# Transposes back on TensorE, key scales also on GpSimd, a six-piece fold and a new instruction order in an RWKV + Fourier-mix kernel

## The chip, the cores and the metric

One Trainium2 chip, one of its cores. The metric is device time in microseconds (us) of one execution, the median over runs. Engines: PE (TensorE: matmuls and transposes; its weight loads are a row of their own, PEld), DVE (VectorE), ACT (ScalarE), POOL (GpSimd), SP (SyncE, which here only issues transfers). DMA engines carry all transfers; SP, ACT and POOL each have a queue that issues them in order.

## The reference

Shapes: batch 4, 8 heads, sequence 768, head size 48, model width 384 (8 x 48), hidden width 1536.

```python
# stage 1: linear attention with a decaying state, per batch and head
cur = np.einsum('bhd,bhe->bhde', u[None] * kt, vt)
y[:, :, t] = np.einsum('bhd,bhde->bhe', rt, state + cur)
state = w[None, :, :, None] * state + np.einsum('bhd,bhe->bhde', kt, vt)
# stage 2: x is y with its heads side by side, 4 x 768 x 384
X = np.fft.fft(np.fft.fft(x, axis=1), axis=2)
u = x + np.real(X).astype(np.float32)
un = (u - mean(u)) / np.sqrt(var(u) + 1e-06)
out = u + np.maximum(un @ w_ch1, 0.0) @ w_ch2
```

## The kernel before

**Stage 1** works on 24 chunks of 128 positions, six to a batch (i = 6b + q). A chunk's keys (and, for batches 1 to 3, its queries) are loaded as f32 into `kr`, its values into `vt`. KR scales keys and queries by powers of the decay (768 elements a partition; K1 is the form for keys alone, 384). V casts the values. The scaled rows have to be turned, so that the head's elements lie on partitions: KRT is the turned tile. For batch 0 PE turns four pairs of heads (tp4; the queries go another way, tp6 and QT6). For later chunks there are two ways: PE with eight transposes into a PSUM bank (tp8) and a copy out of it on ACT or DVE, or one transposing transfer on SP's queue straight from KR to KRT (xbar8), with no PE work and no copy. Then PE makes the scores (A), and each of their two halves is masked, either by ACT's copy AC and POOL's select MA, or by DVE alone (MA); PR multiplies turned keys and queries for the bonus term (PE `de`, ACT DE, TT on POOL or DVE); u and S carry the state; qs, y and X finish the chunk.

**Stage 2**, a batch at a time: the six chunks of X are folded three times (EO: first half of the sequence plus or minus second half; HH: first half of the width plus or minus second; XF: the same with mirrored columns), all on DVE or POOL. For batch 0 the fold runs in thirds, each from two chunks (q and q + 3). Then come PE's first transform fp (four groups g, three parts each), its copy TT2, mirrored copies TR, and the second transform mp with the residual (xr, UF). UB centres the rows, st and MV make the variance. The centred rows have to be turned too (UNT): for the two halves of batch 0 by PE, three transposes for each block of 128 rows (tq) and a copy; for the other six halves by one transposing transfer on SP's queue (xbar9).

**The MLP** takes a half batch (384 rows, hf = 0 to 7) at a time: twelve hp groups of three matmuls 128x384, each followed by HT (ReLU) on ACT or DVE; then for each of three row blocks four mo groups of three matmuls, osb on DVE, and a transfer out. W1 and W2 are loaded and cast by transfers on POOL's queue, three pieces each.

**Order.** Nothing schedules at run time. Each call of `op` appends a numbered operation with its alternatives (engine, form). The list ORDER names every operation once: `1109@4` is operation 1109 on PSUM bank 4, `493.1` operation 493 in its second alternative, a `NONE` alternative emits nothing. One list gives all engines their order; each engine runs its own instructions in that order and waits for what it needs. `idle` operations are matmuls of zeros; as many are emitted as the list names. A tile name such as kr or KR is a ring of buffers (kr has six), handed out in the list's order.

The lines that matter below: L424 KR, L462 tp8, L468 xbar8, L478 PR, L493 A, L502/L505 MA, L661 fp, L736 tq, L753 xbar9, L773 hp, L793 mo, L819 W1, L804/L805 transfers out.

Of the kernel before, what the change touches and what calls it, by code (L numbers as in the profile page):

```python
# [15 lines left out]
H = 8  # L16
S = 768
D = 48
# [9 lines left out]
XBAR_HALVES = frozenset(range(2, 8))  # L28
# [69 lines left out]
211 182.1 188 150 173 151 157 227 171 159 180 155 176.1 229 208 160 187.1 169 167 178 168 231 174.1 158 152@0 161 181  # L98
153 185 156 205 172.1 184 170 162 179 177.1 154 165 163 233 186.1 164 235 215.1 189 196 197 200 212 201 175 216 198
218 166 199 214 190 228 213 192 295 0@1 1@1 2@1 3@1 4@1 5@1 6@1 7@1 8@1 9.1@1 219@1 194 221@2 230 217 297@3 220 313  # L100
225@4 332 315@5 222 232 223@6 351 334@7 226 298.1 353@0 316.1 236 378 224 335 299.2 317.1 10@1 11@1 12@1 13@1 14.2@1
300@1,2 303.1 234 318@5,4 319.1 193 207 210 304.1 307@6 321 301.1 380@3 237 325@1 296 322 320.1 302.1 326 308 314 15@5
16.1@5 17.2@5 305@5 239 306.1 354.1 327 355.2 18@4 19@4 20@4 356@4,2 359.1 202 333 240 309 323 360.1 363@0 328 203 357
206 310.1 248 381 324 311 352.2 364 337@4,2 340.1 336.2 312.1 358 382.2 195 238 21@7 22.2@7 383@7,6 365 341.1 344@3
379 342 345 384 386.1 338.1 390@4 249 405 329.1 330 191 346 407@6 391 242 408 209 392 343 243 183 387.1 361@5 366
362.1 339.1 385 367.1 241 347 368 409.2 331.1 388 393 430 369.1 348.1 293 349 394.1 350.1 245 370 395 389.1 371
410@7,2 413.1 411.1 250 432@6 372.1 414.1 406 415@1 412.1 396.1 244 416 204 23@0 24@0 25@0 418 417.1 373 26@0 27.1@0
419.1 486 420 433 374 28@0 29@0 30.2@0 488@0 376 397 431 246 398 421.1 448 31@2 32.2@2 440@3 489 294 400 33@2 34.1@2
450@5 399 251 377 491@7,4 404 451 375 247 422 811@2 403 823@6 423 492 424 453@1,0 254 402 441.1 425 815@5 401 428 816
449 427 812 429 819@4 426 456 820 434 821 255 813 467 824 825 814 817 822 457 826.1 252 35.1@1 36.2@1 435@1,2 438.1  # L110
487 493 439.1 469@4 818 253 442@6 1062 468 827 829@1 452 494 436.1 830.1 828 257 458 443 454 460@5 437.1 841@7 444 470
842.1 459 463 269 1061 445.1 524 861@0 831.1 867@2 1063 258 477 843.1 490 855@4 856 505 862.1 461 868.1 446 498@1 478
462 507.1@7 857 863.1 832 844 835@0 836 495 526.1@3 508.1 499 447.1 455 501 858 496@4 837 464.1 500 869.1 527.1
510@6,7 511.1 465 513 849@0 509 875@2 502.1 838 512.1 528.1 503 517@3 466.1 851@6 850 853@7 504.1 876 529@5,0 497 870
472@2,1 473.1 854 532 520 852 879@7 474.1 518 506.2 880.1 256 471.1 864 37.2@5 515 534@6 1067@5 1089@1 270 514 530.1
531.1 475 833 1068.1 1069@7 1090 859 519 521 479@0 266 1083@2 1070 834 480 877@5 533 535 516.1 522 1081@1 260 481.1
1084 1077@7 476 878.1 482 483 261 537 525 1065 541 484 1109@4 536 538 267 1079@2 1110 1131@5 1078 542.1 1125@4 1064
539 557 559.2 1129@7 485 560.2 871 1071@0 523 1072 540 263 1075@3 1132 544 1073@0 1130 545 546 1121@6 547 543 1127@5
1122 550 1117@7 632 1082 1123@6 1080 1118 548 1085@1 551 264 1074 549 1087@2 1124 552 1111@7 1128 553 272 575 1126
634@0 1086 1115@6 1076 554 1119@5 262 1088 561.1 577.1@4 259 1066 555 556 273 1112.1 881@1 882 1120.1 883 893@3 894  # L120
265 613 615.2 895 885@2 578.1 635 884 889@0 896 890 891 886 887 616.2 1097@7 888 839 562@5,1 892 580@3,4 897 563 1098
898 860 1116 1113@2 594 596.2 583 899@0 900 920@1 921 1114 579 597.2 569@6 901 581 1091@3 922 570 926@2 927 582 911@0
912 840 268 905@4 906 564 913 932@1 933 1092 558.2 928 565 584 1103@0 845 576 907 587@2 923 566 567@5 1104 846 568 847
571 572 1139@4 902 1105 588 908 651 653.2 585 590 1099 586.1 848 589 591 934 573 1100 914 872 574 617.1 1106 595 919
935 592 1107 604 1093 636.1 593 618@1,6 271 605 1094 621 274 1101 1140 929 622 654.2 1095 625@0 637@2,5 626 619 638.1
598.1 599@1,7 628 614 1145@3 1096.1 600 644@6 627 629 1141 280 940 620 640.1 639.1 602.1 641.1 603.1 623@5 1151@7
624.1 606@2 601 1161@1 1152.1 607 633 275 630 608 915 1146 645 652 631 1163@7 646 1162.1 647 648 281 642 1164 865
1167@0 668.1 643 656@1,7 649 276 669 659 657.1 609 610 655 1173@5 1168 650 660 611 1147 278 866 671 661@1 1171@0 612
662 1174 663 1102.1 664 665 658.1 1153@6 282 1155@2 1108 674 670 284 1201@5 675 1156 666 873 1193@7 1154 667 1165@2
1194 672 285 1207@6 676 1202 673 1195@1 1166 677 679 1208 1159@7 678 287 680 1169@5 681 1133@2 1170 683 279 1142 1160  # L130
682 1172 1134 903 1196 684 686.2 941@6 942 943 949@5 1148 944 721 723.2 687.2 945@7 703 946 1211@0 740 742.2 953@1
1135 288 1212.1 950 951 724.2 1136 952 702 704.2 947 954 955 948 1203@6 874 743.2 1143 956 1209@0 1149 1213@5 688 277
689@7,4 957 958.1 1204 1199@1 290 904 916 759 761.2 1210 1157@3 692 291 1197@6 1200 725.1 1137 1214 980@0 981 959@7
960 1198 286 982 992@1 993 693 1158 696@2 961 1181@5 690 283 994 965@6 966 697 962 691 909 726@0,3 745@7,4 746.1 748.1
685.2 1138.1 729 910 986@1 987 747.1 1144.1 1182 698 699 705.2 924 971@0 972 727 744.1 694@4 967 1183 695.1 988 1175@3
1150 983.1 989 733@6 712 700 749.1 734 1187@1 741.2 995 973 722.2 1176 713.1 1000 730 701 752@7 1188 968 735 1177 974
1189 917 778 780.2 753 979 731 1178 1184 732 754 936 762.2 707@0,2 736 737 706 710 755 756 1190 918 925 937 708 1185
1287@4 781.2 1179 709 1277@0 1191 714@2 728 1215@5 715 289 757 716 1299@3 1216 1186.1 758 717 718 292 1235@1 795.1
1180.1 738 750@5 1236.1 1278 1288 1300 1192.1 796.1 1291@7 739 764@0,4 765.1 711 783@3,1 784.1 766.1 767 786.1 1205@6
763.1 751.1 719 1253@0 720 760 1245@4 801.1 1254.1 1206 1251@2 975 1285@6 785.1 768 1252 769 771@0 1257@2 782 772 1246  # L140
770 773 1247@1 779 963 788@4 1258 774 775 791 964 1229@5 802 789 1292 787.1 790 792 1279@2 976 776 1297@7 1280 777
1248 793 984 1239@3 1298 797.1 794 1217@2 1286.1 1281@0 798.1 1237@1 800 1289@7 799 803 1249@4 805.1 1290 1230 1238
1283@6 1240 806 804 1295@7 807 1218 809 1296 808 1231 810 1243@1 1250.1 1001@3 1002 1284.1 1005@7 1006 1007 1244.1
1013@4 1003 1014 985 969 1015 1009@6 1232 1004.1 1016 1010 1008.1 1011 1223@1 1012 930 1219 1282 931 1017 1241@4 1018
1019@3 1020 1255@7 1021 1025@6 1026 1022.1 1031@0 1032 1027 1220 1033 1224 1028 1046@3 1047 1034.1 938 1242 1225 970
# [22 lines left out]
def kernel(  # L168
# [242 lines left out]
    def attend(i):  # L411
# [449 lines left out]
```

## Time and profile before

| | |
|---|---|
| median of three runs | 174.62 us (173.65 to 176.54) |
| the profiled execution | 176.04 us, its span 174.3 us |
| granted PE clock, mean | 0.997 |
| busy: PE, DVE, ACT, POOL | 160.1, 139.9, 104.5, 71.1 us |
| MLP matmuls (L773, L793) | 2 x 288, 327 and 326 ns mean |
| transposes for KRT on PE (L462) | 64, 220 ns mean |
| transposes for UNT on PE (L736) | 18, 220 ns mean |
| first transform (L661) | 96, 248 ns mean |
| KR, K1 on DVE (L424, L419) | 18 at 1,051 ns, 6 at 547 ns |
| masks on DVE, on POOL (L505, L502) | 23 at 677 ns, 25 at 670 ns |
| PR on DVE, on POOL (L478) | 9 at 409 ns, 9 at 1,166 ns |
| TT on POOL, on DVE (L566) | 22 at 913 ns, 2 at 559 ns |
| V cast on POOL (L434) | 6 at 507 ns |
| KRT copies on ACT, on DVE (1,024 elements) | 5 at 1,050 ns, 3 at 676 ns |
| transposing transfers to KRT, to UNT | 10 at 4.6 us, 6 at 4.5 us to landing |
| loads of K, V, R | 24, 24, 18 of 192 KB; 4.3, 4.1, 4.6 us to landing |

A matmul's mean holds its latency in the pipeline, so the mean is longer than the distance between two of a row; that distance is read from the chain of waits, where a row of matmuls stands as one piece. A PE that is "busy" is therefore not necessarily at work all the time. Instructions of the other engines overlap their neighbours by some 0.06 us.

### The profile page before, as it was taken

How to read it: one execution, taken by the hardware profiler on the slowest of the kernel's cores; microseconds unless marked ns; L12 is line 12 of the kernel's file. 1: busy time of each engine (PE TensorE's matmuls, PEld its weight loads, DVE VectorE, ACT ScalarE, POOL GpSimd, SP SyncE). 2: the span in 40 equal slices, each digit the busy share in tenths (PEclk: the TensorE clock that was granted, in tenths of full speed). 3: DMA queues.
4: the chain of work that ended last, by engine and by line, in shares of the span. 5: the costliest groups of instructions: out<-in, count | busy, mean ns of one | idle time of the engine just before them, and what ended most of it. 6: DMA issues, size and time to landing. Idle time of an engine off the chain costs nothing.

```text
span 174.3 us, 4274 instructions
## 1 busy us (share of the span) xinstructions
PE 160.1 (92%) x1595; PEld 110.8 (64%) x1595; DVE 139.9 (80%) x351; ACT 104.5 (60%) x248; POOL 71.1 (41%) x106
## 2 busy tenths in 40 slices
PE   4888798789999999999999998899999999999991
PEld 1384574578676787677666765567687666666550
DVE  6498999999988998889899899569989975441632
ACT  4968999799984986685657884566433050423000
POOL 8605760178962125997300596876200001100110
PEclk9999999999999999999999999999999999999998
DMA  5999798999999999999999899870001604210323
GB/s 139 289 202 207 152 220 208 239 188 212 207 168 204 172 133 220 130 209 217 230 223 154 187 246 244 120 201 4 0 0 30 177 8 104 95 45 0 125 101 137
DMA packets 91558, 26.79 MB, mean 154 GB/s; under 512 B 86977, under 2 KB 90178, under 8 KB 91538
## 3 DMA queue, kind: packets, MB, share of 16 engines
q1 hardware_dynamic: 89568, 22.19, 65.4%
q0 software_dynamic: 1440, 3.74, 10.1%
q10 hardware_dynamic: 530, 0.59, 0.9%
q8 instruction: 12, 0.20, 0.5%
q14 instruction: 8, 0.07, 0.1%
HBM read 19.77 MB, written 4.72 MB: 140 GB/s over the span
## 4 chain that ended last, share of the span: by engine, by line
PE 58%; DMA 14%; DVE 12%; issue 5%; POOL 5%; ACT 3%; SPq 1%; DVEq 0%; ACTq 0%; POOLq 0%
PE bank L773 22%; PE bank L793 21%; DMA W<-in_moe_w_ch_dram 5%; DMA HT<-in_r_dram 3%; PE bank L661 3%; DMA KRT<-KR 3%; DMA kr<-in_r_dram 3%; PE bank L700 2%; POOL TT L566 2%; PE bank L493 2%; PE bank L578 2%; DVE HH L609 2%; DVE MA L505 2%; PE bank L384 1%; DVE KR L424 1%
## 5 line engine op out<-in xcount | busy, mean ns | idle before, releaser
L773 PE MATMUL bank<-early,W 128*128 128x384 bf16 x288 | 55.0, 327 | 0.3 <-DMA W<-in_moe_w_ch_dram 0.2
L793 PE MATMUL bank<-W,HT 128*128 128x384 bf16 x288 | 54.4, 326 | 0.0
L778 ACT ACTIVATE HT<-bank 128x384 bf16<-128x384 f32 x71 | 31.1, 501 | 24.7 <-PE bank L773 24.7
L773 PEld LDWEIGHTS <-W 128*128 128x128 bf16 x288 | 30.8, 114 | 13.2 <-DMA W<-in_moe_w_ch_dram 0.5
L793 PEld LDWEIGHTS <-HT 128*128 128x128 bf16 x288 | 26.8, 98 | 14.7
L566 POOL TENSOR_TENSOR TT<-V,DE 128x384 bf16<-128x384 bf16 x22 | 19.9, 913 | 7.7 <-ACT DE L565 4.0
L502 POOL TENSOR_SCALAR_AFFINE_SELECT MA<-AC 128x512 bf16<-128x512 bf16 x25 | 16.4, 670 | 14.8 <-ACT AC L500 10.6
L800 DVE SCALAR_TENSOR_TENSOR osb<-bank,rstd,UF 128x384 f32<-128x384 f32 x24 | 13.9, 610 | 9.7 <-PE bank L793 9.6
L804 POOL DMA_DIRECT2D out_dram<-osb x7 | 3.9, 556 | 43.2 <-DVE osb L800 43.2
L424 DVE TENSOR_TENSOR KR<-kr,wtab 128x768 bf16<-128x768 f32 x18 | 18.8, 1051 | 0.9 <-DMA kr<-in_r_dram 0.9
L779 DVE TENSOR_SCALAR HT<-bank 128x384 bf16<-128x384 f32 x25 | 13.2, 550 | 7.6 <-PE bank L773 6.9
L478 POOL TENSOR_TENSOR PR<-KRT 128x512 bf16<-128x512 bf16 x9 | 10.4, 1166 | 20.3 <-DMA KRT<-KR 20.2
L500 ACT CAST AC<-bank 128x512 bf16<-128x512 f32 x25 | 14.6, 594 | 6.5 <-PE bank L493 4.2
L505 DVE TENSOR_TENSOR MA<-bank,mtri 128x512 bf16<-128x512 f32 x23 | 15.0, 677 | 0.7 <-PE bank L493 0.6
L719 ACT ACTIVATE UB<-UF,sm 128x384 bf16<-128x384 f32 x20 | 12.0, 614 | 3.3 <-DVE UF L712 3.2
L726 DVE BATCH_NORM_STATS2 st<-UF 128x6 f32<-128x384 f32 x24 | 12.9, 546 | 0.0
L586 DVE TENSOR_TENSOR X<-bank,TT 128x384 bf16<-128x384 f32 x15 | 8.3, 550 | 4.7 <-PE bank L578 4.7
L661 PE MATMUL bank<-te_t,XF 128*128 128x193 bf16 x96 | 10.4, 248 | 0.8 <-DVE XF L624 0.8
L284 PE MATMUL bank<-zero 128*128 128x512 bf16 (+2 forms) x38 | 10.5, 398 | 0.6 <-DVE PR L481 0.5
L712 DVE SCALAR_TENSOR_TENSOR UF<-bank,X 128x384 f32<-128x384 f32 x20 | 10.5, 545 | 0.7 <-PE bank L700 0.7
L669 ACT CAST TT<-bank 97x386 bf16<-97x386 f32 x13 | 7.3, 600 | 6.2 <-PE bank L661 6.1
L661 PEld LDWEIGHTS <-XF 128*128 128x128 bf16 x96 | 8.0, 98 | 2.8 <-DVE XF L624 1.4
(113 smaller groups left out, 256.1 us busy)
## 6 DMA issues: line engine op xcount, KB each, us to landing
kr<-in_k_dram SPq DMA_DIRECT2D x24, 192.0 KB, 4.3
vt<-in_v_dram SPq DMA_DIRECT2D x24, 192.0 KB, 4.1
kr<-in_r_dram SPq DMA_DIRECT2D x18, 192.0 KB, 4.6
out_dram<-osb SPq DMA_DIRECT2D x17, 192.0 KB, 2.1
W<-in_moe_w_ch_dram POOLq DMA_DIRECT2D x6, 384.0 KB, 6.1
out_dram<-osb POOLq DMA_DIRECT2D x7, 192.0 KB, 2.3
te_t<-te_c SPq DMA_DIRECT2D x1, 579.0 KB, 5.1
HT<-in_r_dram SPq DMA_DIRECT2D x1, 576.0 KB, 4.1
```

The lines of the kernel that those rows point to most:

```text
L424: one(("KR", i), "DVE", "KR", lambda: nc.vector.tensor_tensor(out=KR().rearrange("t s p (a d) -> t (s p) a d", a=2)[:, :, :, 0:D], in0=kr( ...
L500: op(("AC", i, a), [("ACT", "AC", lambda: nc.scalar.copy(AC(), A_ps[a]())), ("NONE", "", None)], r=[("A", i)], w=[("AC", i, a)], new=[AC], ...
L502: op(("MA", i, a), [("POOL", "MA", lambda: nc.gpsimd.affine_select(out=MA[a](), in_=AC(), pattern=[[0, NP], [1, 128]], base=0, channel_mul ...
L505: ("DVE", "MA", lambda: nc.vector.tensor_tensor(out=MA[a](), in0=A_ps[a](), in1=mtri.unsqueeze(1).to_broadcast([128, NP, 128]), op=AluOp.m ...
L566: op(("TT", i), [(e, key, lambda g=g: g.tensor_tensor(out=TT(), in0=V(), in1=DE().unsqueeze(2).to_broadcast([128, H, D]), op=AluOp.mult)) ...
L661: nc.tensor.matmul(fp()[:, par, :], lhsT=XF()[:, par, nb, g * CH:g * CH + 128], rhs=te_t[:, g % 2, nb, par, :], start=(nb == 0 and par == ...
L726: one(("st", b, blk), "DVE", "st", lambda: nc.vector.bn_stats(out=st(), in_=UF()[:, j, :]), r=[("UF", b, blk)], new=[st], use=[UF])
L773: nc.tensor.matmul(hp(), lhsT=W1[:, dt, ft // 4 * 512:(ft // 4 + 1) * 512].rearrange("k (m j) -> k m j", j=4)[:, :, ft % 4], rhs=UNT()[:, ...
L778: op(("HT", hf, ft), [("ACT", "HT", lambda: nc.scalar.activation(out=HT()[:, ft, :], in_=hp(), func=Act.Relu, scale=-1.0)), ("DVE", "HT", ...
L779: ("DVE", "HT", lambda: nc.vector.tensor_scalar(out=HT()[:, ft, :], in0=hp(), scalar1=-1.0, scalar2=0.0, op0=AluOp.mult, op1=AluOp.max))],
L793: nc.tensor.matmul(mo(), lhsT=HT()[:, ft, j * 128:(j + 1) * 128], rhs=W2[:, ft, :], start=(ft == 0), stop=(ft == 11))
L800: one(("osb", hf, j), "DVE", "osb", lambda: nc.vector.scalar_tensor_tensor(out=osb(), in0=mo(), scalar=rstd()[:, j:j + 1], in1=UF()[:, j, ...
```

## The change

Five things change in the code, and the order list is new.

1. The transposing transfers go: KRT has only its two copies from PSUM, tp8 is always issued, and all eight halves of the MLP rows are turned by tq.
2. KR can run on POOL as well, whole (KRg, K1g), or be split into keys and queries on two engines (KR and KR2).
3. UB can run on POOL (UBg).
4. Batch 0's fold has no sequence step EO. Each chunk q is folded over the width alone as soon as it is there (HHn, then XFn, two instructions each, six times). The plus and minus over the sequence halves is left to PE: the first transform now sums six parts in place of three, the last three with the table `te_t` or its negated odd part `tn_t`, which one instruction (`tn`) makes. EO and HH of the other batches can run on DVE only.
5. The ring kr has five buffers for six.

```diff
-XBAR_HALVES = frozenset(range(2, 8))
...
+    tn_t = const([128, 2, 3, 193], BF16, "tn_t")
...
-    ring("kr", 6, [128, 2, H, D], F32)
+    ring("kr", 5, [128, 2, H, D], F32)
...
+        def scaled(g, s):
+            return g.tensor_tensor(
+                out=KR()[:, s].rearrange("t p (a d) -> t (p a) d", a=2)[:, :, 0:D], in0=kr()[:, s],
+                in1=wtab[ph][:, s].rearrange("t (h d) -> t h d", d=D), op=AluOp.mult)
...
+            op(("KR", i), [(e, key, lambda g=g: scaled(g, 0)) for e, key, g in (("DVE", "K1", nc.vector), ("POOL", "K1g", nc.gpsimd))],
...
+            op(("KR", i), [("DVE", "KR", lambda: both(nc.vector)), ("DVE", "K1", lambda: scaled(nc.vector, 0)),
+                           ("POOL", "K1g", lambda: scaled(nc.gpsimd, 0)), ("POOL", "KRg", lambda: both(nc.gpsimd))],
+               r=need, w=[("KR", i)], new=[KR], use=[kr])
+            op(("KR2", i), [("NONE", "", None), ("POOL", "K1g", lambda: scaled(nc.gpsimd, 1)),
+                            ("DVE", "K1", lambda: scaled(nc.vector, 1)), ("NONE", "", None)],
...
-            op(("tp", i), [("PE", "tp8", transposes), ("PE", "tp8", transposes), ("NONE", "", None)], r=[("KR", i), "ident"],
-               w=[("tp", i)], new=[tp], uses=[[KR], [KR], []])
+            one(("tp", i), "PE", "tp8", transposes, r=[("KR", i), ("KR2", i), "ident"], new=[tp], use=[KR])
...
-                            ("SP", "xbar8", lambda: nc.sync.dma_start_transpose(
-                                out=KRT().rearrange("d s p t -> d (s p) t"), in_=KR().rearrange("t s p c -> t (s p c)")))],
...
+    def narrow(q):
+        X, HHt, XF = bat[0]["X"], bat[0]["HH"], bat[0]["XF"]
+        e, n = divmod(q, 3)
+        def hid(h, alu):
+            op(("HH", 0, q, h), [(en, "HHn", lambda g=g: g.tensor_tensor(
+                out=HHt()[:, h, e, n, 0:192], in0=X()[:, q, 0:192], in1=X()[:, q, 192:384], op=alu))
...
+        def sym(h, alu):
+            grp = (slice(0, 4, 3), slice(1, 3, 1))[h]
+            op(("XF", 0, q, h), [(en, "XFn", lambda g=g: g.tensor_tensor(
+                out=XF()[:, e, n, 0:4 * CH].rearrange("t (g c) -> t g c", g=4)[:, grp], in0=HHt()[:, :, e, n, 0:CH],
+                in1=HHt()[:, :, e, n, 192:192 - CH:-1], op=alu)) for en, g in (("DVE", nc.vector), ("POOL", nc.gpsimd))],
...
+                        e, n = divmod(nb, 3)
+                        lhsT, rhs = XF()[:, e, n], (tn_t[:, g % 2, n, :] if e and par else te_t[:, g % 2, n, par, :])
...
+                ("POOL", "UBg", lambda: nc.gpsimd.tensor_scalar(
+                    out=UB()[:, j, :], in0=UF()[:, j, :], scalar1=-float(DM), scalar2=sm()[:, j:j + 1], op0=AluOp.mult,
...
-            if 2 * b + sh in XBAR_HALVES:
-                one(("UNT", b, sh), "SP", "xbar9", lambda UB=UB, UNT=UNT: nc.sync.dma_start_transpose(
...
+            for j in range(3):
+                turned(sh, j, UB, UNT)
...
+    op("tn", [("ACT", "tn", lambda: nc.scalar.mul(tn_t, te_t[:, :, :, 1, :], -1.0)),
```

The two order lists, with each number traced to its operation and alternative, hold (operations before -> after):

| operation | all | ahead of the first hp |
|---|---|---|
| PE tp8 (8 transposes), tq (3) | 8 -> 18, 6 -> 24 | 6 -> 6, 5 -> 6 |
| PE fp (2 matmuls), xr | 48 -> 60, 4 -> 5 | 12 -> 24, 4 -> 5 |
| PE y, qs, de | 24, 20, 24, as before | 9 -> 11, 8 -> 10, 11 -> 12 |
| PE idle | 38 -> 25 | 38 -> 25 |
| DVE KR, K1 | 18 -> 9, 6 -> 1 | 6 -> 3, 6 -> 1 |
| POOL KRg, K1g | 0 -> 9, 0 -> 5 | 0 -> 3, 0 -> 5 |
| MA on DVE, on POOL | 23 -> 29, 25 -> 19 | 13 -> 20, 7 -> 3 |
| PR and PRp on DVE, PR on POOL | 14 -> 21, 10 -> 3 | 9 -> 12, 3 -> 0 |
| DVE EO, HH, HHn, XFn | 18 -> 18, 21 -> 18, 0 -> 10, 12 -> 11 | 6 -> 0, 5 -> 0, 0 -> 10, 12 -> 11 |
| POOL EO, HH, HHn, XFn | 6 -> 0, 3 -> 0, 0 -> 2, 0 -> 1 | 0, 1 -> 0, 0 -> 2, 0 -> 1 |
| DVE KRT, S, TR, QT6 | 3 -> 10, 10 -> 9, 7 -> 2, 0 -> 2 | 2 -> 4, 5 -> 2, 2 -> 0, 0 -> 2 |
| DVE UNT copies, TTd, UB, UF, X, st | 4 -> 9, 2 -> 3, 4 -> 5, 20 -> 19, 15, 24 | 4 -> 2, 1 -> 2, 0 -> 1, 2 -> 1, 0 -> 1, 0 -> 1 |
| POOL UBg, TT | 0 -> 9, 22 -> 21 | 0 -> 1, 8 -> 9 |
| transfers out on SP, on POOL | 17 -> 13, 7 -> 11 | none |

Ahead of the first hp, SP's queue has K0 to K4 behind one half of batch 0's queries before; after, it has K0 and V0 ahead of that half. The third piece of W1 stands in POOL's queue directly behind KRg of chunk 11. The first MLP operations are hp (0,7), (0,10), then (0,0).

## The prediction

> **What bounds the kernel now.** I read the slices first, then the stretches, then the chain of waits from the first MLP matmul on, then the groups and single instructions of the stage ahead of it.
>
> ```profile
> PE   4888798789999999999999998899999999999991
> PEclk9999999999999999999999999999999999999998
> DMA  5999798999999999999999899870001604210323
> ```
>
> TensorE (PE) is full from the eleventh slice (44 us) to the last, at its full clock; the DMA engines are full for the first 29 slices.
>
> ```profile
> 20.00:30.00 10.00, 9.15 (x140) 6.10 (x139) 9.70 (x22) 9.29 (x22) 3.54 (x5) 1.00 0.89 197
> 30.00:40.00 10.00, 8.38 (x111) 6.52 (x111) 9.83 (x29) 8.98 (x21) 4.58 (x6) 1.00 1.04 208
> 40.00:47.00 7.00, 6.57 (x121) 5.09 (x118) 7.00 (x18) 6.72 (x19) 6.78 (x9) 1.00 1.12 215
> 47.00:60.00 13.00, 12.74 (x115) 9.21 (x115) 11.46 (x28) 9.67 (x27) 4.69 (x7) 1.00 1.08 178
> 60.00:80.00 20.00, 19.57 (x240) 14.70 (x239) 17.75 (x44) 15.44 (x37) 14.36 (x19) 1.00 1.10 181
> 80.00:100.00 20.00, 19.78 (x198) 13.99 (x197) 18.32 (x46) 13.71 (x33) 5.20 (x8) 1.00 1.03 200
> 100.00:120.00 20.00, 18.46 (x212) 12.63 (x210) 16.36 (x38) 12.53 (x34) 15.39 (x20) 1.00 0.92 180
> ```
>
> After the stretch and its length the columns are busy us of PE, weight loads, DVE, ACT, POOL, then clock, DMA share and GB/s. From 20 to 47 us DVE is busy 26.53 of 27 us: it sets the pace there. From 47 us on PE is, idle only 0.26 + 0.43 + 0.22 + 1.54 = 2.45 us up to 120 us and not at all from there to 169.95 us.
>
> ```profile
> 39.10 8.08 DMA W<-in_moe_w_ch_dram
> 47.23 1.33 PE bank L773 x7
> ...
> 60.28 0.45 PE bank L462 x8
> 60.72 2.05 PE bank L661 x24
> ...
> 108.74 4.94 DMA KRT<-KR
> ...
> 158.73 11.23 PE bank L793 x69
> ```
>
> Start, length, what: the chain crosses from the W1 load to PE at 47.23 us and stays mostly on PE. Here stand PE's issue prices, free of the latency in the groups' means: 11.23/69 = 0.163 us for an MLP matmul (0.49 a group of three), 0.45 for eight transposes (0.056 each), 2.05/24 = 0.085 for a fold matmul (0.17 a group of two).
>
> The first MLP matmul (order group hp) starts at 46.57 us, the last ends at 169.95: 123.4 us. By such prices the PE order holds from there on 192 MLP groups (94.1 us), 36 fold groups (6.2), 18 mp x 0.33 (5.9), 12 A x 0.28 (3.4), 15 y x 0.20 (3.0), 12 qs x 0.18 (2.2), ten state updates (2.1), 13 bonus groups x 0.10 (1.3), two tp8 (0.9) and one tq (0.17): **119.2 us of work, 4.2 of gaps**. What counts is when the first MLP matmul starts, what PE still has to do then, the gaps, and the tail (174.30 - 169.95 = 4.35 us).
>
> **The change part by part.**
>
> *Transposes back on PE.* Ten tp8 x 0.45 = 4.5 us and eighteen tq x 0.17 = 3.0 us. All ten tp8 and seventeen tq (2.8) stand behind the first MLP matmul. There nothing hides them, PE being full. The new order also puts two y, two qs and one bonus group, 0.86 us, ahead of that point. Remaining PE work: 119.2 + 4.5 + 2.8 - 0.9 = **125.6 us, +6.4**.
>
> The row for these transposes is 0.45 us for eight at a granted clock of 1.00. [...]
>
> *First fold in six narrow pieces.* Twelve fold groups more, 2.05 us of PE, and one more xr (0.16), all ahead of the first MLP matmul. PE's order has 22.9 us of work there now, in 46.6 us, and 26.2 after; thirteen idle matmul groups (38 to 25) make room. DVE's pace hides it; without that cover it is 3.2 us.
>
> *DVE ahead of the first MLP matmul.* By the groups' means: less KR 3 x 1.051 and K1 5 x 0.547 (-5.9, to POOL), EO 6 x 0.377 and HH 5 x 0.389 (-4.2), S, TR, UF, UNTj (-3.6); more HHn 10 x about 0.257 (as XFn, 196 elements; +2.6), MA 7 x 0.677 (+4.7), KRT 2 x 0.676 (+1.4), PR and PRp 3 x 0.41 (+1.2), two QT6 (about 0.5 each, from KRT's 0.676 for 1,024 elements), and TTd, UB, X, st (+2.2). Small rest -0.1. Net **about -0.7 us**: the scales leave, masks take their place. ACT gets about 2 us lighter, with one tn of about 1.1 (1,158 elements against KRT's 1.05 for 1,024).
>
> *W1.* These loads sit in POOL's queue, which now holds five K1g, three KRg and fewer MA and PR ahead of the third piece. K1g and KRg have no row. Bounds: the V cast, 507 ns for 384 elements with one input, gives 1.0 for KRg's 768; PR's 1,166 ns for 512 with two inputs gives 1.75. I take 1.75, and 0.9 for K1g (TT, 913 for 384). The last KRg is directly ahead of the third W1 piece; behind it wait that load, the TT of chunks 7 to 10 and then the first MLP matmul. In the shared order that piece has moved behind some 1.6 us more DVE work. Today it is issued at 39.1 and lands at 47.2, when PE is just ready. I take +1.2 us for the first MLP matmul; bounds -1 (DVE 0.7 lighter, and POOL done with its scales in time) and +3 (one KRg late on its load too).
>
> [...]
>
> *Gaps.* The ten KRT and six UNT transfers (4.6 and 4.5 us to landing) leave the DMA queue. What PE can win is bounded by the gaps: 1.5 of its idle time names KRT transfers. Against that DVE gets tighter: from the first MLP matmul to the last batch's fold it has about 74 us of work against PE's 77 (67.5 against 74.5 before). And POOL slows DVE:
>
> ```profile
> 34.14 2.13 POOL L502 TENSOR_SCALAR_AFFINE_SELECT MA<-AC 128x512 bf16<-128x512 bf16 x2 [7.86 <-ACT AC L500]
> ...
> 34.40 1.38 DVE L424 TENSOR_TENSOR KR<-kr,wtab 128x768 bf16<-128x768 f32 x1
> ```
>
> Two masks took 2.13 where a pair takes 1.22 elsewhere, and the KR beside them 1.38 where others take 0.95: 0.43 us for a collision. Fourteen scales on POOL could cost DVE 0 to 6 us; most would fall in its 3 us of slack. I take -1.5 for the transfers and +1.5 for this: gaps unchanged, bounds -3 and +4.
>
> *At nothing:* UBg on POOL (nine, about 0.5, replacing ACT's 0.614), TR moved to ACT (0.83 against 0.35, eight in all), the shorter kr ring (five for six; the load order hides it while K and R arrive at 200 GB/s; a late load costs one kr transfer, 4.6 us), outputs between SP and POOL. UNT copies need banks and 18 x about 0.4 us of ACT or DVE, inside ACT's free time.
>
> Sum on the span: 174.3 + 6.4 + 1.2 + 0 = 181.9. The profiled execution took 176.04, 1.74 around its span, and would become 183.6; the median lies 1.42 under it. **Prediction: 174.62 + 7.6 = 182.2 us.**
>
> **The rivals.**
>
> *1. The gaps close* (12%). With no transfer to wait for, the gaps fall from 4.2 to about 1 and the first MLP matmul is on time: 174.62 + 6.4 - 3.2 = 177.8, within 2%. For it: POOL's 20.2 us of waiting for KRT. Against: PE itself waited only 1.5 us of that.
>
> *2. The first MLP matmul comes early: not slower* (8%). DVE idles 0.91 + 1.54 + 1.25 + 0.58 = 4.3 us up to 13.8 us, waiting for queries and their tables, and POOL scaling keys beside it could fill this. If all of it went and the gaps closed too, 174.62 + 6.4 - 4.3 - 3.2 = 173.5. It decides from 6.4 us up, for which both must succeed; to be 2% faster needs 9.9 us, more than both bounds. Against: K0 and V0 now stand ahead of SP's query load, which the DVE idle of 1.25 waits for.
>
> *3. POOL becomes late* (8%). Its in-order queue holds KRg in front of TT and MA; if six KRg behind the first MLP matmul each delay a score chain by 1 us that PE cannot fill, 182.2 + 6 = 188.
>
> That the transposes would not move to PE is ruled out by the decoded order.
>
> **How the numbers follow.** Forecast 72%, rivals 12, 8 and 8. The 2% that a measurement can tell is 3.5 us: 171.1 to 178.1. Faster takes most of rival 2 for what rows of one execution cannot bound (6%); same is rival 1 and the rest of 2 (14%); slower is the forecast and rival 3 (80%). The forecast alone spans 178 to 187 (bounds of start and gaps, not all at once). The range takes in rival 1 and part of 2 below and most of rival 3 above: 175.5 to 188, leaving out some 15%.
>
> **What would show it.** The tp8 line should count 144 transposes and the tq line 72, at 0.056 us of issue each; PE's work from the first MLP matmul on 125 to 126 us; that matmul at 46 to 49 us; KRg at 1.6 to 2.1 us; POOL's waits for KRT gone. The forecast falls if the first MLP matmul starts before 43 us or if PE's end minus that start is under 122 us.

## The result and the profile after

The kernel after takes **182.22 us** (median of 4 runs, 181.99 to 183.76), the kernel before, beside it, 174.55 (4 runs): ratio **1.048, 95% interval 1.040 to 1.056**, slower. The profiled execution took 182.13 us with a span of 180.3 us; the spans differ by 6.0 us, the medians by 7.7, because the profiled execution of before lies 1.5 us above its median. Executions of one kernel lie 2 to 9 us apart, in part with a lower mean granted clock and in part without one (the kernel before took 174.47 and 177.98 us at 1.00), so ratios and intervals compare the faster executions (two to four of each new kernel; where only one was left, no ratio is given), and the clock stands beside a time where it matters.

The slices of the kernel after (4.5 us each):

```profile
PE   3976888849999999999999999999999999999991
PEclk9999999997999999999999999999999999999998
DMA  5999899999989589978712210110010201200333
```

PE is full from the tenth slice on (40.6 us), but the ninth holds a 4, an idle time, and in the tenth the clock has a dent. The DMA engines are nearly idle from the twenty-first slice on (before: from the twenty-eighth; the prediction read them as full for 29 slices, they are for 27), because the turns have left them and the loads are earlier.

The stretches, with the columns of the prediction:

```profile
30.00:40.00 10.00, 7.41 (x106) 6.01 (x104) 9.93 (x18) 7.65 (x18) 7.19 (x7) 1.00 1.06 203
40.00:47.00 7.00, 6.30 (x81) 5.31 (x80) 5.92 (x13) 4.54 (x16) 2.80 (x5) 0.76 1.12 216
47.00:60.00 13.00, 12.62 (x147) 9.54 (x143) 12.51 (x30) 10.57 (x28) 4.36 (x5) 1.00 0.93 182
60.00:80.00 20.00, 20.00 (x265) 15.65 (x264) 18.85 (x49) 18.41 (x42) 16.24 (x20) 1.00 0.97 187
80.00:100.00 20.00, 20.00 (x209) 14.13 (x208) 18.15 (x50) 12.55 (x28) 9.94 (x12) 1.00 0.47 112
100.00:120.00 20.00, 20.00 (x252) 15.27 (x250) 18.90 (x47) 11.37 (x32) 13.64 (x21) 1.00 0.13 49
```

From 60 to 120 us PE is busy 60.00 of 60 us (57.81 before). Before 47 us it is worse off: 7.41 of 10 us against 8.38, and then 7 us at a clock of 0.76.

The chain of waits:

```profile
37.08 2.96 DVE PR L490
...
49.68 1.14 PE bank L792 x6
...
60.72 0.45 PE bank L477 x8
...
162.42 14.15 PE bank L812 x87
```

The first MLP matmul starts at 49.68 us (46.57 before), the last ends at 176.56, and 3.69 us follow. In the kernel before the last one ends at 170.43, and 3.90 us follow:

```profile
167.82 2.60 PE L793 MATMUL bank<-W,HT 128*128 128x384 bf16 x15
```

The prediction's 169.95 is where the chain of waits leaves PE, 0.5 us ahead of its last matmul; so the stretch before was 123.9 us with 4.7 of gaps, not 123.4 with 4.2, and the tail 3.90, not 4.35. A turn of keys, L477, is 0.45 us for eight on the chain, as it was; an MLP matmul 14.15/87 = 0.163. By the prediction's prices the new order holds 125.6 us of work behind the first MLP matmul; the stretch is 126.9, so the gaps, which are the stretch less the priced work, are 1.3 us. In spans: first MLP matmul +3.1, work +6.4, gaps -3.4, tail -0.2, together +5.9.

The groups that the change touches:

```profile
L477 PE MATMUL bank<-ident,KR 128*128 128x128 bf16 x144 | 11.4, 224 | 0.5 <-DVE KR L432 0.5
L760 PE MATMUL bank<-ident,UB 128*128 128x128 bf16 x72 | 7.4, 219 | 0.0
L432 POOL TENSOR_TENSOR KR<-kr,wtab 128x768 bf16<-128x768 f32 x9 | 17.2, 1907 | 0.0
L432 DVE TENSOR_TENSOR KR<-kr,wtab 128x768 bf16<-128x768 f32 x9 | 8.5, 966 | 0.0
```

144 and 72 transposes, as decoded. POOL's whole scale takes 1.91 us, twice DVE's 0.97.

Why the first MLP matmul is late shows in single instructions of DVE and POOL:

```profile
36.41 0.67 DVE L517 TENSOR_TENSOR MA<-bank,mtri 128x512 bf16<-128x512 f32 x1
37.00 3.04 DVE L490 TENSOR_TENSOR PR<-KRT 128x512 bf16<-128x512 bf16 x1
39.96 1.28 DVE L517 TENSOR_TENSOR MA<-bank,mtri 128x512 bf16<-128x512 f32 x2
...
36.74 1.18 POOL L841 DMA_DIRECT2D W<-in_moe_w_ch_dram  x2
37.94 1.81 POOL L432 TENSOR_TENSOR KR<-kr,wtab 128x768 bf16<-128x768 f32 x1
39.69 0.57 POOL L841 DMA_DIRECT2D W<-in_moe_w_ch_dram  x1
...
40.70 0.49 PE L721 MATMUL bank<-hid_t,TR 97*128 97x192 bf16 x4 [2.53 <-DVE MA L517]
```

A PR that takes 0.41 us elsewhere takes 3.04 and ends 0.3 us behind POOL's scale of chunk 11. The masks behind it free the banks that PE's next group needs: PE idles 2.53 us up to 40.70. W1's third piece was issued at 39.69 and nothing waited for it.

### The profile page after: what moved, and what is told of

It reads as the page before. It is cut to its first block, busy times and chain, and to the rows that moved or that the text cites. A ratio compares the mean times of both kernels' runs of the same rounds, so it can differ in the third digit from the quotient of the medians.

```text
span 180.3 us, 4560 instructions
## 1 busy us (share of the span) xinstructions
PE 165.5 (92%) x1741; PEld 118.5 (66%) x1741; DVE 147.2 (82%) x372; ACT 106.3 (59%) x251; POOL 79.2 (44%) x110
## 4 chain that ended last, share of the span: by engine, by line
PE 75%; DVE 16%; DMA 3%; issue 2%; ACT 1%; SPq 1%; DVEq 0%
PE bank L792 26%; PE bank L812 26%; DVE MA L517 5%; PE bank L721 4%; PE bank L477 4%; PE bank L682 4%; DMA HT<-in_r_dram 3%; PE bank L505 2%; DVE PR L490 2%; PE bank L760 2%; PE bank L591 2%; DVE KR L432 1%; PE bank L574 1%; DVE W L378 1%; DVE XF L621 1%
## 5 line engine op out<-in xcount | busy, mean ns | idle before, releaser
L823 POOL DMA_DIRECT2D out_dram<-osb x11 | 6.3, 574 | 47.5 <-DVE osb L819 42.8
L514 POOL TENSOR_SCALAR_AFFINE_SELECT MA<-AC 128x512 bf16<-128x512 bf16 x19 | 12.3, 655 | 21.0 <-ACT AC L512 17.8
L517 DVE TENSOR_TENSOR MA<-bank,mtri 128x512 bf16<-128x512 f32 x29 | 18.9, 679 | 0.5 <-PE bank L505 0.4
L432 POOL TENSOR_TENSOR KR<-kr,wtab 128x768 bf16<-128x768 f32 x9 | 17.2, 1907 | 0.0
L682 PE MATMUL bank<-te_t,XF 128*128 128x193 bf16 x108 | 12.6, 248 | 0.8 <-ACT X L601 0.4
L512 ACT CAST AC<-bank 128x512 bf16<-128x512 f32 x19 | 10.8, 598 | 4.1 <-PE bank L505 2.1
L477 PE MATMUL bank<-ident,KR 128*128 128x128 bf16 x144 | 11.4, 224 | 0.5 <-DVE KR L432 0.5
L477 PEld LDWEIGHTS <-KR 128*128 128x128 bf16 x144 | 9.3, 100 | 1.4 <-DVE KR L432 0.6
L448 ACT CAST V<-vt 128x384 bf16<-128x384 f32 x19 | 9.7, 516 | 0.7 <-PE bank L591 0.7
L287 PE MATMUL bank<-zero 128*128 128x512 bf16 (+2 forms) x25 | 7.6, 411 | 2.5 <-DVE PR L493 1.4
```

What stands on the lines that cost most here:

```text
L432: return g.tensor_tensor(out=KR().rearrange("t s p (a d) -> t (s p) a d", a=2)[:, :, :, 0:D], in0=kr().rearrange("t s (p a) d -> t (s p) a ...
L477: nc.tensor.transpose(tp()[:, s, p, :], KR()[:, s, p, :], ident)
L514: op(("MA", i, a), [("POOL", "MA", lambda: nc.gpsimd.affine_select(out=MA[a](), in_=AC(), pattern=[[0, NP], [1, 128]], base=0, channel_mul ...
L517: ("DVE", "MA", lambda: nc.vector.tensor_tensor(out=MA[a](), in0=A_ps[a](), in1=mtri.unsqueeze(1).to_broadcast([128, NP, 128]), op=AluOp.m ...
L682: nc.tensor.matmul(fp()[:, par, :], lhsT=lhsT[:, g * CH:g * CH + 128], rhs=rhs, start=(nb == 0 and par == 0), stop=(nb == last and par == ...
```

## The experiments

Each kernel was timed beside the kernel before, whose median was 176.1, 176.4, 176.8 and 175.9 us in the four sets; ratios compare best. "Stretch" is from the first MLP matmul to the end of the last, "idle" PE's idle time in it, both of the profiled execution: 123.9 and 2.4 before, 126.9 and 0.3 after. (Idle counts only time in which no matmul stands in the profile; the gaps above count all time that the prices do not explain.)

**PE work alone** (`before_more_pe`): the kernel before with 6.4 us of matmuls of zeros added behind the first MLP matmul, a 160-column one in each of 96 mo groups.

```diff
+                if ft == lo:
+                    nc.tensor.matmul(mo()[:, 0:160], lhsT=zero[:, 0:128], rhs=W2[:, ft, 0:160], start=False, stop=False)
```

> The kernel before, with one matmul of zeros of 160 columns added to each of the 96 second MLP groups (the sums stay the same). By the prices 160 columns cost 0.067 us, so PE gets 6.4 us more work behind the first MLP matmul and nothing else changes. Theory 'work' (PE is full there, the change's 6.4 us of work is its loss): +6.4 us on the kernel before, about 181. Rival 'gaps' (the 4.2 us of gaps take the work up, the loss came with the late start and with POOL): +2.2 us at most, under 177.

183.03 us, ratio 1.037 (1.026 to 1.047), which on 174.55 is +6.4 us (4.6 to 8.3). Stretch 130.1, 6.3 longer, idle 2.7. PE's work is on the path one for one, and the gaps do not close because PE has more to do: what waits in the order of before waits as long.

**The turns doubled** (`turns_twice`): the kernel after with the ten added tp8 and eighteen added tq issued twice.

```diff
-                for s in range(2):
+                for _ in range(2 if i in (12, 14, 15, 17, 18, 19, 20, 21, 22, 23) else 1):
...
-                for dt in range(3):
+                for _ in range(2 if b else 1):
```

> The changed kernel, with the turns that the change brought to PE (ten groups of eight, eighteen groups of three) made twice into the same bank. Theory 'work': 10 x 0.45 + 18 x 0.17 = 7.5 us more, about 189.7. [...]

191.94 us, ratio 1.089 (1.073 to 1.105), 0.042 or 7.3 us above the ratio of after (the two intervals leave some 4 to 10). Sharper is the stretch: 133.9, 7.0 more than after, for 134 transposes, 0.052 us each. Nothing hides a turn in this order, and none costs more than its row said.

**One scale back on DVE** (`kr11_on_dve`): chunk 11's keys and queries, whose scaling on POOL held PR.

```diff
-... 530.3 531.3 ...
+... 530 531 ...
```

> The changed kernel, with the scale of chunk 11 on DVE in its old form. In the changed kernel one PR on DVE (37.00 us) took 3.04 us, others 0.41; on POOL two W1 issues, this KRg and the third W1 issue ran meanwhile. Theory 'KRg holds DVE': the PR falls to 0.4 to 1.5 us, DVE gains 2.6 less 0.9 for the scale, the first MLP matmul comes about 2 to 3 us earlier and the time falls by as much, to about 179.5. Rival 'the W1 issue holds DVE': the PR stays over 1.5 us long, the time rises by up to 0.9.

185.24 us (180.56 to 185.69), no ratio; the profiled execution took 180.56 at a granted clock of 1.00, the other three ran at 0.972 to 0.977. The same instructions as above:

```profile
37.39 0.40 DVE L490 TENSOR_TENSOR PR<-KRT 128x512 bf16<-128x512 bf16 x1
37.72 1.27 DVE L517 TENSOR_TENSOR MA<-bank,mtri 128x512 bf16<-128x512 f32 x2
...
37.13 1.71 POOL L841 DMA_DIRECT2D W<-in_moe_w_ch_dram  x3
```

PR is 0.40 us beside the W1 issues: these do not hold it, the scale on POOL does. First MLP matmul 48.17 us, 1.5 earlier where 2 to 3 was expected, stretch 126.9. The time as a whole is not settled by these four runs.

**The turns back on transfers, in the new order** (`turns_by_dma`): each transfer where its copy stood.

```diff
-            op(("KRT", i), [("ACT", "KRT", lambda: nc.scalar.copy(KRT(), tp())),
+            op(("KRT", i), [("ACT", "KRT", turn_by_dma if xbar else lambda: nc.scalar.copy(KRT(), tp())),
...
+                if len(seen) == 3:
+                    nc.sync.dma_start_transpose(out=UNT().rearrange("p j c t -> p (j c) t"), in_=UB().rearrange("p j d -> p (j d)"))
```

> The changed kernel, with the same ten KRT and six UNT as before turned by transfers on SP's queue, at the places of their copies in the unchanged order. Theory 'work': PE loses 7.5 us of work, ACT and DVE their copies; the transfers take 4.6 us where turn and copy took about 1.5, and the order was not made for that, so of 7.3 us it keeps 3 to 7: 175 to 179. Rival 'gaps': no gain, 182 or more.

201.37 us, ratio 1.148 (1.137 to 1.159): the expectation missed by over 20 us. PE's waits:

```profile
PE bank L803 <- DMA early<-UB: 16.9, 4, 10.2
```

Four transfers of centred rows (tile `early`) cost 16.9 us, one of them 10.2. The new order leaves a turn no time to travel, so the old turns cannot simply be put into it.

**The turns on PE, in the old order** (`before_turns_on_pe`): the ten KRT by tp8, the six UNT by nine transposes and two copies, at the places of their transfers.

```diff
-... 559.2 ... 560.2 ...
+... 559@0 560.0 ...
...
-                one(("UNT", b, sh), "SP", "xbar9", lambda UB=UB, UNT=UNT: nc.sync.dma_start_transpose(
+                one(("UNT", b, sh), "PE", "tq9", half, r=[("UB", b, sh * 3 + j) for j in range(3)], new=[UNT] + pair, use=[UB])
```

> The kernel before, in its own order, with the ten KRT and six UNT that it turned by transfers turned by TensorE instead (thirty tp8 lines of transposes in all, eighteen tq; copies on ScalarE, a third of each UNT's on VectorE); all scaling on VectorE, fold in three pieces. Theory 'the turns are the loss': TensorE's work after the first MLP matmul grows by about 7.5 us (80 and 54 transposes of 0.056 us), of which at most about 2.5 us of the gaps closes: 179.5 to 182.5 us, ratio 1.03 to 1.045. Rival 'the new order and the late start are the loss, the turns fill the gaps': 175 to 178 us, ratio under 1.02. Third: the copies that now follow each turn on ScalarE and VectorE push the casts and stalls come on top: over 183 us.

194.28 us, ratio 1.101 (1.089 to 1.114), 0.053 or some 9 us above after. Stretch 140.7, idle 10.4. PE now waits for the copies:

```profile
PE bank L781 <- ACT KRT L467: 4.1, 4, 1.1
...
PE bank L701 <- ACT KRT L467: 1.7, 2, 1.1
PE bank L494 <- ACT KRT L467: 1.6, 2, 1.1
...
PE bank L556 <- ACT KRT L467: 1.1, 1, 1.1
```

It is the third theory of the expectation. Turns on PE do not fill gaps by themselves; they make new ones, unless the order gives each copy its time. To a kernel that turns on PE, the rest of the change is worth some 9 us: the new order, with the GpSimd scales and the narrow fold, which this experiment leaves out and does not tell apart.

**All key scales of GpSimd back on DVE** (`kr_scale_on_dve`): nine KRg moved, the five K1g and nine UBg left.

```diff
-... 450.3 451.3 ... 490.3 491.3 ... 530.3 531.3 ...
+... 450 451 ... 490 491 ... 530 531 ...
```

> The kernel after with all nine scalings of keys that GpSimd does (1.91 us each) put back on VectorE (1.1 us each for three, 27 halves or so), the rest of its GpSimd work (K1, centred rows) as it is. Theory 'a VectorE instruction with two SBUF inputs is held while GpSimd scales keys': the PR that took 3.04 us takes 0.41, first MLP matmul at 47.5 to 48.5 us; VectorE gets some 8.5 us more work in all, and since it is not full it costs no more than 1 us after the first MLP matmul: total 180 to 182 us. Rival 'GpSimd is the help that closed the gaps': the gaps go from 1.3 us back to 3 or more and the total is 183 to 186 us.

185.66 us (182.74 to 185.98), no ratio; the profiled execution, at a clock of 1.00, took 182.74. First MLP matmul 48.25 us, as the first theory said (PR is not held here either); but the stretch is 129.0 with 1.3 idle, 2.1 us longer than with POOL's help:

```profile
60.00:80.00 20.00, 18.80 (x236) 14.12 (x235) 19.89 (x49) 16.84 (x37) 11.30 (x17) 1.00 1.06 203
```

DVE is busy 19.89 of 20 us there and PE loses 1.2. The scales on POOL cost the start something and give about 2 us back behind it.

**The narrow fold alone** (`before_six_piece_fold`): the kernel before with the six-piece fold.

```diff
-    ring("kr", 6, [128, 2, H, D], F32)
+    ring("kr", 5, [128, 2, H, D], F32)
...
+    def narrow(q):
```

> The kernel before, in its own order, with the first fold in six narrow pieces instead of three (tn and the scaled keys in five buffers, for space). Prediction's step: the fold's extra 2.05 us of TensorE work lies in time that waits anyway, VectorE gains about 1.3 us ahead of the first pair, ScalarE 1.1 us more: ratio 0.99 to 1.01. Rival 'the narrow fold delays the first pair, and through it the first MLP matmul': first MLP matmul 1 to 2 us later than 46.6, ratio 1.01 or more.

179.29 us, ratio 1.012 (0.994 to 1.029): not settled. In its profile the first MLP matmul is at 49.27 us, but the chain runs through the place that this edit gave `tn`:

```profile
23.04 5.97 DMA te_t<-te_c
29.03 1.17 ACT tn_t L829
```

ACT waited for the table's load at 29 us, which the kernel after, with `tn` elsewhere, does not. PE was busy for 0.30 of the 2 us from 28 us on, and the clock has a dent from 31.7 to 35.1 us. One execution at clock 1.00 took 176.67. What the fold costs alone stays open, between -1 and +5 us.

**Idle time filled, first try** (`after_kept_warm`): ten more idle matmuls ahead of the group that waits, in bank 6.

```diff
-... 441.1 385.1 404 ...
+... 25@6 26@6 27@6 28@6 29@6 30@6 31@6 32@6 33@6 34@6 ...
```

> The kernel after, with ten more of its idle matmuls on zeros (0.216 us each) ahead of the third head-pair group, where TensorE idled 2.53 us before 40.70 us. Theory 'the idle time lowered the granted clock to 0.76 in 40 to 47 us': the clock is back to 0.95 or more there, and the first MLP matmul comes 1 to 1.6 us earlier (48 to 48.7 us), total 180 to 181.5 us. Rival 'the held VectorE row alone sets it': clock or no clock, the first MLP matmul stays at 49 to 50 us and the total at 182 to 183 us.

187.34 us (182.18 to 190.28), no ratio. The edit missed its aim: bank 6 was itself held by a mask behind the held PR (2.98 us on the chain here), so the ten ran after the wait, 3.62 us of them at half clock on the chain, and the first MLP matmul came at 57.08; 3.4 us of that lateness is older: on the chain PR starts at 40.46 us here and at 37.08 in the kernel after, and this profile has another dent in the clock from 16.5 us on.

**Idle time filled, second try** (`idle_filled`): the same ten in bank 0, which is free ahead of PE's wait.

```diff
+... 25@0 26@0 27@0 28@0 29@0 30@0 31@0 32@0 33@0 34@0 ...
```

> The kernel after, with ten more idle matmuls on zeros (0.22 us each), this time into a bank that is already free, between two groups that TensorE issues ahead of its wait of 2.53 us. Theory 'that idle time lowers the granted clock afterwards': the clock in 40 to 47 us is 0.95 or more in every profile, the mean granted clock of the executions rises from 0.981-0.991 to 0.99 or more, first MLP matmul 48 to 48.8 us, total 180 to 181.5 us. Rival 'the clock falls for another reason, and the held VectorE row alone delays': the clock's mean and the total (182 to 183 us) stay.

181.69 us, ratio **1.032 (1.025 to 1.039)**, below the interval of after; four executions at a clock of 0.997 to 1.00 took 180.5 to 182.0, two at 0.981 took 185.6. On PE and by stretch:

```profile
37.46 2.32 PE L288 MATMUL bank<-zero 128*128 128x512 bf16 x10
39.62 0.61 PE L478 MATMUL bank<-ident,KR 128*128 128x128 bf16 x8
```

```profile
40.00:47.00 7.00, 6.75 (x132) 5.67 (x129) 6.42 (x14) 6.33 (x23) 4.62 (x7) 1.00 1.12 215
```

The dent in the clock is gone and the first MLP matmul is at 48.08 us. This profile does not tell clock from hold: POOL's scale of chunk 11 was itself waiting for its load (0.49 us), and PR took 0.42. Two other profiles do. `turns_twice` has the same PE instructions up to the first MLP matmul, the same held PR (2.96 us on the chain, as there) and the same idle time, but its clock stays at 1.00 from 40 us on:

```profile
44.90 0.49 PE L722 MATMUL bank<-hid_t,TR 97*128 97x192 bf16 x4 [2.53 <-DVE MA L518]
...
52.57 1.14 PE L794 MATMUL bank<-early,W 128*128 128x384 bf16 x6
```

From the end of the wait to the first MLP matmul it needs 7.67 us, the kernel after 8.98. And in `late_keys_by_dma` (below), which has the ten idle matmuls, PR is held too, PE is busy for 6.59 of the 7 us from 40 to 47 us, and the clock stays at 1.00:

```profile
41.08 3.05 DVE L496 TENSOR_TENSOR PR<-KRT 128x512 bf16<-128x512 bf16 x1
```

So the hold does not make the dent by itself, and the dent costs 1.3 us. What the hold costs beside it: from the PE group L721 ahead of the wait (36.87 us in the kernel after) to the first MLP matmul it is 12.8 us with hold and dent, 11.5 with the hold alone, and 10.9 in `kr11_on_dve` with neither.

**The keys alone by transfers** (`keys_by_dma`), each issued where its transposes stood.

```diff
-            one(("tp", i), "PE", "tp8", transposes, r=[("KR", i), ("KR2", i), "ident"], new=[tp], use=[KR])
+            one(("tp", i), "PE", "tp8", (lambda: None) if xbar else transposes, r=[("KR", i), ("KR2", i), "ident"], new=[tp], use=[KR])
```

In this kernel and in the next, one of twenty state products (qs of chunk 14) reads the tile KRT after a later chunk has taken it, so that part of the output is another and that matmul waits for the later turn.

> The kernel after, with the ten KRT alone turned by transfers (each issued where its transposes stood), the UNT on TensorE as in the change. TensorE's work falls by 80 transposes of 0.056 us, 4.5 us. Theory 'the turned keys cost 4.5 us, and their transfers fit because the transfers' load falls to 0.13 after 100 us': TensorE's stretch from the first MLP matmul on is 122 to 123.5 us, gaps under 1.5 us, total 177 to 179 us. Rival 'the transfers are late again, so the turns by TensorE were worth their price': gaps of 3 us or more, total 181 us or more.

202.76 us, ratio 1.131 (1.120 to 1.141): the rival. Nearly all of it is one transfer:

```profile
72.11 1.58 SPq L483 DMA_TRANSPOSE KRT<-KR  x1
...
72.39 1.14 POOL L849 DMA_DIRECT2D W<-in_moe_w_ch_dram  x2
...
88.77 0.76 DVE L496 TENSOR_TENSOR PR<-KRT 128x512 bf16<-128x512 bf16 x2 [16.39 <-DMA KRT<-KR]
```

```profile
76.00:80.00 4.00, 0.00 (x0) 0.00 (x0) 0.00 (x0) 0.00 (x0) 1.65 (x3) 0.77 1.42 97
80.00:84.00 4.00, 0.00 (x0) 0.00 (x0) 0.00 (x0) 0.00 (x0) 0.00 (x0) 0.50 1.20 44
```

The three W2 loads are issued within 3.6 us from 72.4 us on, and the turn issued among them lands after 16 us while the DMA engines are full (a share of 1.20) at 44 GB/s. In the kernel before, the W2 pieces go out apart, at 48.9, 52.8 and 61.5 us, and a turn lands in 4.6 at the median; the one issued at 51.1, between two pieces, took 9.2.

**The same with scale 11 on DVE** (`keys_by_dma_kr11`): both edits above together.

```diff
-... 530.3 531.3 ...
+... 530 531 ...
```

> The same as the kernel with the keys by transfers, and also the scaling of keys 11 on VectorE instead of GpSimd, so that PR is not held for 3 us ahead of the first MLP matmul. Theory 'both parts add up': first MLP matmul 47.7 to 48.5 us, total 1.5 us under the kernel with the keys by transfers, 175.5 to 177.5 us, still not under the kernel before. Rival 'what GpSimd's scaling holds back returns elsewhere': the same time as the kernel with the keys by transfers.

201.63 us, ratio 1.139 (1.130 to 1.148): no difference that can be told from the one before. The late transfer stands ahead of everything; idle is 16.6 us.

**Only the late keys by transfers** (`late_keys_by_dma`): the second filled kernel with KRT of chunks 18 to 23 turned by transfers, behind the W2 loads and ahead of the stores in SP's queue. Here qs of chunk 19 reads a later chunk's keys.

```diff
-            one(("tp", i), "PE", "tp8", transposes, r=[("KR", i), ("KR2", i), "ident"], new=[tp], use=[KR])
+            xbar = i in (18, 19, 20, 21, 22, 23)
```

> The kernel with the idle time filled, and the last six KRT (18 to 23) turned by transfers, each issued when its scaled keys are done and ahead of the stores that SyncE waits for; these lie behind the three W2 loads, beside which a transfer of keys took 16 us to land in the kernel with all ten by transfers. TensorE's work falls by 48 transposes of 0.056 us, 2.7 us. Theory 'turned keys cost TensorE 0.45 us a chunk, and a transfer is free only where no large load runs beside it and it is issued early': stretch from the first MLP matmul 124 to 125 us (126.9 with all turns on TensorE), gaps under 1 us, total 178 to 179.5 us where the kernel with the idle time filled took 181.7. Rival 'transfers of keys cannot be fitted into this order anywhere': gaps of 3 us or more and 182 us or longer.

183.27 us, ratio 1.033 (1.026 to 1.040), the ratio of the filled kernel: no gain. Idle plus work is 126.1 us: 2.6 us less work as expected, 1.8 us more idle, and a tail 0.8 us longer. PE's new wait, 1.7 of the 1.8 us:

```profile
PE bank L688 <- DVE XF L656: 1.7, 1, 1.7
```

The transfers land in time (3.8 us), most of the saving goes into this wait for the fold's XF. Executions at the full clock took the same in both: 180.77 against 180.51 us. Between the two theories: the transfers fit, and the time is not had.

None of these kernels is faster than the kernel before.

## Why the prediction was right, by its steps

**PE's work, +6.4 us: right.** Counts and issue distances came as read off; adding 6.4 us of other matmuls cost 6.4, doubling the turns 7.3. The rows have 224 ns for one transpose, and yet 134 more of them added 0.052 us each. As a price in a full row the rows' mean does not serve.

**Gaps unchanged: wrong in size.** The step "-1.5 for the transfers and +1.5" for collisions should have read -3.4 (-2.9 by the prediction's own reading of the end, at its bound of -3). Rival 1 had said 4.2 would fall to about 1, and 1.3 is left. They did not close because PE has more to do (`before_more_pe`, idle 2.7), nor because the turns are on PE (`before_turns_on_pe`, 10.4): it took an order that places the copies, and DVE's scales on POOL, whose return costs 2.1 us. The collisions that were feared did not grow behind the first MLP matmul: DVE's rows that are over 0.15 us longer than the shortest of their form add 2.2 us there (3.2 before). The large one, PR's 2.6 us, fell ahead of it.

**First MLP matmul, +1.2 us: mis-sized, at +3.1, and its reason false.** It lies just outside the bound of +3 and the 46 to 49 us named as a sign. It was argued from W1's third piece behind POOL's scale; W1 was in time. What failed is "DVE about -0.7", and a clock taken at 1.00, as every stretch of before from 20 us on has it. Up to the first MLP matmul DVE worked 44.9 us against 41.2: PR was held for 2.6 us, and the two QT6 took 0.95 each where about 0.5 was assumed (a small constant, `icol`, took 1.56 for 0.16, but ahead of a wait for a load, where it costs nothing). Of the +3.1, the comparisons above put 1.3 on the dent in the clock and 0.6 on the hold, net of the scale that `kr11_on_dve` has on DVE in its place. The 1.2 that is left happens to be the forecast's size, but it is not shown to be its cause: the start of one kernel moves by as much from execution to execution. The profile of `before_more_pe`, the same code up to there, reaches the first MLP matmul at 45.39 us, 1.2 ahead of the profile of before, whose PE was still slower between 10 and 12 us (last section); behind the wait for W1 that follows (0.92 us there, 0.17 in the kernel before) 0.4 us of the lead is left.

**The narrow fold, hidden: open.** The one test of it had a flaw of its own.

**Tail 4.35: 3.69.** Read rightly it was 3.90 before; no change worth a term.

The total was met by luck: gaps 3.4 us better than forecast, start 1.9 worse and tail 0.2 better leave the spans 5.9 us apart where 7.6 was forecast, and the medians happen to lie 1.7 further apart than the spans.

**The rivals.** Rival 1's gaps came, its start on time did not. Rival 2 (early start) and rival 3 (POOL late) did not happen. KRg at 1.91 us was 0.16 over the row taken; it is 1.97 times DVE's 0.97. The 2.1 at the upper end of its sign is shown by no run; eight of the nine took 1.81 to 1.83 us, and one 2.61.

## What to carry to other kernels

Where an engine is full in the stage that sets the end, price what is moved onto it by its issue distance in a row, one for one, and do not expect it to be hidden (here 6.4 us of matmuls cost 6.3 to 6.4, and 134 turns 0.052 us each). A transfer and an order belong together: the turns by transfer left PE idle for 2.4 us in the order that issued them early and kept loads apart, and for 19 us in one that did not; the turns on PE cost some 9 us more with the old order. Before moving two-input work to GpSimd, look at which DVE instruction will stand beside it, and who waits for that one (here a PR of 3.04 us for 0.41, and PE for 2.53).

## What the runs showed of the hardware

**After an idle time of PE the granted clock dropped to half for 3.41 us, in some profiles.** In the kernel after, in stretches of 1 us, PE having idled from 38.16 to 40.70:

```profile
41.00:42.00 1.00, 1.00 (x18) 0.73 (x16) 1.00 (x3) 0.60 (x3) 0.00 (x0) 1.00 1.19 233
42.00:43.00 1.00, 1.00 (x9) 0.90 (x8) 1.00 (x3) 1.00 (x6) 0.00 (x0) 0.69 1.05 200
43.00:44.00 1.00, 1.00 (x14) 0.99 (x13) 0.83 (x3) 1.00 (x4) 0.84 (x2) 0.50 1.17 226
44.00:45.00 1.00, 1.00 (x15) 0.83 (x14) 0.46 (x1) 0.51 (x3) 0.77 (x1) 0.50 1.12 213
45.00:46.00 1.00, 1.00 (x16) 0.79 (x16) 1.00 (x3) 0.79 (x3) 0.00 (x0) 0.60 1.06 204
46.00:47.00 1.00, 1.00 (x23) 0.76 (x21) 0.62 (x2) 0.64 (x2) 0.93 (x2) 1.00 1.16 233
```

The dent comes late, when PE is busy again (3.41 of 3.41 us), and lasts 3.41 us. The clock records of the two traces lie on a grid: in the kernel after full clock is recorded from 8.26 us on, half clock from 42.39 and full clock again from 45.80, ten steps of 3.413 us and one, and in the kernel before full clock from 12.80 and half clock from 173.23, 47 steps. By the stretches of 2 us eight other profiles have dents of 3.4 us, of 6.8 in `after_kept_warm` and `keys_by_dma`, and of 10.2 and twice 17.1 over PE's long waits (10.2 us in `turns_by_dma`, 15.3 in `keys_by_dma`, 8.5 in `keys_by_dma_kr11`). Worked out from these stretches, the dents of `turns_by_dma` begin at 15.8, 43.1, 73.8 and 128.4 us: 8, 9 and 16 steps of 3.41 us apart. Cut into such steps, from 12.80 us on in the kernel before and 8.26 in the kernel after, the two traces hold 94 windows at full clock that have another behind them. In 93 PE's rows cover 0.60 or more, and full clock follows; in the one that half clock follows, 38.97 to 42.39 us in the kernel after, they cover 0.50. The length of an idle time alone does not decide: PE's wait for the mask, 2.5 us each time, was followed by a dent in the kernel after, in `turns_by_dma` and in `keys_by_dma`, and not in `turns_twice`. By its dents at 16.5 and 26.8 us an edge of the grid of `turns_twice` falls at 43.8, into its wait (42.37 to 44.90). That the place on the grid decides is the author's estimate from these windows, not shown. The same kernel dips in one execution and not in another: `kr11_on_dve` took 180.56 us at 1.00 and 185.69 at 0.972, and 0.028 of its span of 183.8 us is 5.1. (The 4 us between executions of the kernel before are not from this; its clock was 0.99 to 1.00.)

At the start of a kernel the clock column does not tell the speed. The traces of the kernels before and after have no record ahead of 12.80 and 8.26 us, and the column prints 1.00, but ten matmuls of zeros take 4.23 us in the kernel before, and 2.32 later on in `idle_filled` (above):

```profile
3.77 4.23 PE L284 MATMUL bank<-zero 128*128 128x512 bf16 x10
```

In the profile of before the first record of full clock is at 12.80 us; that of `before_more_pe` was faster ahead of that: from 10 to 12 us its 27 weight loads took 1.45 us, the 20 of the kernel before 2.00. Transposes did not keep the full clock away: from 9.52 us to that record the kernel before ran transposes alone, 3.28 us of them.

**Beside POOL's whole scales, two of three DVE instructions with two SBUF inputs were held.** In the kernel after PR took 3.04 us for 0.41 and EO 1.64 for 0.32, both to the end of a scale on POOL; PR took 3.05 in `late_keys_by_dma`, and on the chain 2.96 to 2.98 in `turns_twice`, `turns_by_dma` and `after_kept_warm`. A mask with an input from PSUM took its usual 0.67 beside one. DVE's own scale at 22.16 us, 0.01 ahead of POOL's, took its usual 0.95, and POOL's took 2.61 for 1.82. PR was held from 0.94 us before the scale's own row begins, while POOL still issued W1 ahead of it; where the scale was not next in POOL's queue, or waited for its load, PR took 0.40 and 0.42 beside the same issues.

**A turning transfer beside large loads** took 16 us to land in `keys_by_dma`, where 4.6 is the median in the kernel before, at 44 GB/s with the DMA engines full (a share of 1.20). In the kernel before the one issued at 51.09 us, with the W2 pieces of 48.91 and 52.77 under way, took 9.2, and the fifteen others 2.9 to 5.3; on the chain of `turns_by_dma` one took 11.0 and four others 2.8 to 4.3. What in the loads delays them is not shown.
